# How 64-bit weights become 32-bit ones in the opening of a one-core light-convolution and maxout kernel: low bits on ScalarE or GpSimd

## The chip, the cores and the metric

One Trainium2 chip, one core, one program. The metric is device time in microseconds: before the change the median of 3 runs is 1399.69 us (1399.49 to 1399.96). PE is TensorE (PEld its weight loads), DVE is VectorE, ACT is ScalarE, POOL is GpSimd, SP is SyncE, which issues the DMAs.

## The reference

Two stages, one after the other. The first is a light convolution: for each of 8 x 4160 tokens and each of 8 heads, 7 weights go through a softmax and mix the token with the 6 before it (192 features, 24 per head). The second is a maxout layer: `h = max(x @ w1, x @ w2, x @ w3)` with 192 x 768 weights, then `out = h @ w_out` with 768 x 192. The four weight matrices come as 64-bit floats; tokens and convolution weights are 32-bit.

## The kernel before

**Tiling.** The 33,280 tokens are 65 chunks of 512, each 4 tiles of 128. 192 features are a first part of 128 rows (names with a) and a second part of 64 (names with b). 768 hidden features are 6 blocks `j`, taken as 3 pairs `jp`. Per chunk the kernel makes four tap products and their sums (`taps`: L522 on POOL or, for the tiles of TAPS_ON_VECTOR, on DVE; the sums L535 on DVE), turns the tokens so that features lie in the partitions, splits them into a high and a low part (`parts`), multiplies with the weights (`up`), takes the maximum (`evict`) and multiplies with w_out (`down`). So that the maximum needs only two products, x @ w1 is taken out of it and added at the end through a composed matrix `wc = w1 @ w_out` (`compose`); `up` uses the differences `w2 - w1` and `w3 - w1` (`differences_a`, `differences_b`), a relu (L1389) and a maximum (L1397, L1406).

**Two ways to multiply.** Chunk 0 uses full 32-bit matmuls (`up_whole`, L1349 and L1356; `down_whole`, L1436 to L1445), which need no split weights. From chunk 1 on, weights and tokens are high and low parts and the two halves of 64 rows of the array work side by side (`products`, L1287). The low parts of the weights are made by `rest` (L1004), of w_out at L1129; xb, a low part of the tokens, at L723.

**64-bit to 32-bit** (`single`, L814 on). Twelve pieces: for each pair ('a', jp, 0) with 256 columns (w1), ('a', jp, 1) with 512 (w2, w3), ('b', jp) with 384 (the last 64 rows of all three), and ('d', q) with 384 (w_out). ACT takes the high words' absolute value (L832) into a PSUM bank, or into a buffer `m` in SBUF if POOL clamps; a clamp follows, on DVE or POOL (L849) or as two scalings on ACT (L842); then three DVE passes: shift left by 3 (L856), join the sign from the high word (L865), join the low word shifted right by 29 (L874). In the last two, one input is the word in SBUF and the other the value in the bank:

```
nc.vector.scalar_tensor_tensor(
    target().bitcast(U32), low(), 29, ui(),
    op0=ALU.logical_shift_right, op1=ALU.bitwise_or,
)
```

**Last 64 rows.** `differences_b` writes the high part of a pair to `bhi` (L1089), in whose 128 partitions the even and the odd block lie in a half each, and four ACT copies (L1108) put each block into both halves of `wb_hi`, because both halves of the array need it.

**Composing.** `compose(0)` makes the first 128 rows of wc, `compose(1)` the last 64, each by six matmuls added up in one bank (L1181; each is recorded as two passes); copies on ACT (L1193, L1203, L1213, L1232) and a subtraction on DVE (L1220) make the parts.

**Order of the work.** The program is written by a planner in Python: each instruction is a task with an engine, a cost, predecessors, buffers it holds and a due time; per engine the ready task with the earliest time goes first. TensorE's tasks alone keep the order of the program. For chunks 0 and 1 that order is the list OPENING, written by hand: loads, softmax, conversions (`singles`), taps, 'warm' (matmuls of the identity, L898, each unit 128 columns, which fill the time until data is there), 'turn x' (tokens, L576, L613), 'turn' (weights, L1156, L1157), 'a' and 'b' (differences, L1017, L942), 'up', 'compose' and 'down'. LOAD_DUE sets when the loads are due, and a table of shifts in `Plan(...)` moves the times of single tasks. MODE, CLAMP_ON_POOL, CLAMP_ON_SCALAR and ON_POOL_FIRST say which engine makes a difference, a clamp or a low part.

## Time and profile before

| | |
|---|---|
| runs | 1399.69 us median of 3 (1399.49 to 1399.96) |
| profiled execution | 1399.97 us |
| its span, first to last instruction | 1398.1 us |
| granted clock of TensorE, mean | 0.999 |
| PE, PEld busy | 1391.6, 1327.1 us |
| DVE, ACT, POOL busy | 1009.5, 1128.3, 1094.8 us |

The page gives busy shares for the whole span; waits, timelines, windows and groups are asked of the trace for one engine or stretch. The end of a matmul is modelled, so of PE the starts are read, not the lengths. Times in a view count from the span's start.

### The profile page before, as it was taken

Reading aid. Unit: us, or ns where it says so; the run is one execution under the profiler, and the core shown is the slowest. Engines: PE = TensorE matmul, PEld = TensorE weight load, DVE = VectorE, ACT = ScalarE, POOL = GpSimd, SP = SyncE. Lnnn points to the kernel's source line nnn. Section 1 sums busy time; section 2 is a strip of 40 time slices with the busy share of each in tenths; the row PEclk is TensorE's granted clock in tenths of the full one; section 3 lists DMA queues with packets and bytes.
Section 4 is the critical chain, followed back from the end, with each engine's and each line's share of the span. In section 5 each row is a group of like instructions: output and inputs, shape, how many; then the busy total and the mean of one; then the engine's idle time right before and its main releaser. Section 6 shows DMA issues by size and latency. Waiting matters only on the chain.

```text
span 1398.1 us, 36944 instructions
## 1 busy us (share of the span) xinstructions
PE 1391.6 (100%) x14825; PEld 1327.1 (95%) x14825; DVE 1009.5 (72%) x1373; ACT 1128.3 (81%) x2870; POOL 1094.8 (78%) x606
## 2 busy tenths in 40 slices
PE   9999999999999999999999999999999999999998
PEld 4899999999999999999999999999999999999998
DVE  7988777677677678668668667668767768767533
ACT  6687888788888888888788888888888888789773
POOL 7999998788788788788788788788788788788321
PEclk9999999999999999999999999999999999999999
DMA  7202211011111011111011111011111111110000
GB/s 245 104 19 105 75 58 70 25 60 69 70 60 69 24 59 70 70 59 70 24 59 70 70 59 70 26 57 70 70 59 70 38 55 60 56 63 19 24 24 24
DMA packets 23532, 85.68 MB, mean 61 GB/s; under 512 B 2632, under 2 KB 9544, under 8 KB 19520
## 3 DMA queue, kind: packets, MB, share of 16 engines
q1 hardware_dynamic: 23360, 83.32, 16.2%
q8 instruction: 116, 1.90, 0.6%
q14 instruction: 56, 0.46, 0.1%
HBM read 57.75 MB, written 25.56 MB: 60 GB/s over the span
## 4 chain that ended last, share of the span: by engine, by line
PE 92%; DVE 2%; POOL 2%; ACT 1%; DMA 1%; issue 1%; SPq 0%; DVEq 0%; POOLq 0%; ACTq 0%
PE bank L1287 92%; POOL r L522 1%; DVE acc L535 1%; ACT room L688 1%; DMA h_lo<-in_moe_w_dram 0%; POOL h_lo L1417 0%; DMA h_hi<-in_moe_w_dram 0%; DVE h_hi L1397 0%; DVE bank L865 0%; DVE bank L856 0%; PE bank L1265 0%; ACT m L1389 0%; POOL xb L723 0%; POOL wt L485 0%; DVE r L522 0%
## 5 line engine op out<-in xcount | busy, mean ns | idle before, releaser
L522 POOL TENSOR_TENSOR r<-xt,wt 128x1344 f32<-128x1344 f32 x257 | 714.2, 2845 | 139.1 <-DVE acc L535 137.1
L1287 PE MATMUL bank<-wo,h_hi 64*128 64x384 f32 x3060 | 657.4, 356 | 0.0
L1287 PE MATMUL bank<-wo,h_lo 64*128 64x192 f32 x3060 | 584.5, 247 | 0.0
L688 ACT COPY room<-room 32x128 f32<-32x128 f32 x1512 | 448.6, 297 | 61.4 <-DVE room L677 38.3
L1287 PEld LDWEIGHTS bank<-wo,h_lo 64*128 64x128 f32 x3060 | 480.4, 187 | 0.0
L1287 PEld LDWEIGHTS bank<-wo,h_hi 64*128 64x128 f32 x3060 | 471.5, 185 | 0.0
L1287 PE MATMUL bank<-xa_hi,wa_hi 64*128 64x512 f32 x1536 | 459.0, 389 | 0.0
L1287 PE MATMUL bank<-xa_lo,wa_hi 64*128 64x512 f32 x1536 | 455.6, 387 | 0.0
L1287 PE MATMUL bank<-xa_hi,wa_lo 64*128 64x512 f32 x1536 | 455.1, 387 | 0.0
L535 DVE TENSOR_REDUCE acc<-r 128x192 f32<-128x1344 f32 x257 | 399.6, 1556 | 5.2 <-POOL r L522 4.3
L1287 PE MATMUL bank<-xc,wb_hi 64*128 64x512 f32 x768 | 276.8, 386 | 0.0
L1389 ACT ACTIVATE m<-bank 128x512 f32<-128x512 f32 x390 | 232.4, 597 | 54.3 <-PE bank L1287 48.5
L1287 PE MATMUL bank<-xb,wb_hi 64*128 64x512 f32 x768 | 271.6, 387 | 0.0
L1287 PE MATMUL bank<-xc,wb_lo 64*128 64x512 f32 x768 | 250.5, 386 | 0.0
L1287 PEld LDWEIGHTS bank<-xa_hi,wa_hi 64*128 64x128 f32 x1536 | 239.6, 184 | 9.1 <-issue 0.2
L1287 PEld LDWEIGHTS bank<-xa_lo,wa_hi 64*128 64x128 f32 x1536 | 239.5, 184 | 8.9
L1287 PEld LDWEIGHTS bank<-xa_hi,wa_lo 64*128 64x128 f32 x1536 | 238.9, 184 | 9.2
L1528 DVE TENSOR_TENSOR o<-bank,ob 128x192 f32<-128x192 f32 x255 | 89.0, 349 | 187.7 <-ACT ob L1521 187.5
L1417 DVE TENSOR_TENSOR h_lo<-bank,h_hi 128x512 fp32r<-128x512 f32 x254 | 174.1, 685 | 59.6 <-ACT h_hi L1410 59.1
L1417 POOL TENSOR_TENSOR h_lo<-m,h_hi 128x512 fp32r<-128x512 f32 x130 | 171.1, 1317 | 39.4 <-ACT h_hi L1410 39.2
L1406 DVE TENSOR_TENSOR bank<-bank,m 128x512 f32<-128x512 f32 x254 | 175.4, 691 | 16.2 <-ACT m L1389 10.3
L1287 PE MATMUL bank<-wca,xa_hi 64*128 64x384 f32 x510 | 179.4, 352 | 0.3 <-SPq L1293 0.3
(132 smaller groups left out, 2046.7 us busy)
## 6 DMA issues: line engine op xcount, KB each, us to landing
xt<-in_x_dram SPq DMA_DIRECT2D x30, 1344.0 KB, 5.8
out_dram<-o SPq DMA_DIRECT2D x64, 384.0 KB, 2.3
wt<-in_weight_gen_dram SPq DMA_DIRECT2D x31, 224.0 KB, 2.5
xt<-in_x_dram SPq DMA_DIRECT2D x2, 960.0 KB, 6.6
h_hi<-in_moe_w_dram SPq DMA_DIRECT2D x6, 256.0 KB, 4.6
xt<-in_x_dram SPq DMA_DIRECT2D x2, 768.0 KB, 5.0
room<-in_moe_w_out_dram SPq DMA_DIRECT2D x2, 384.0 KB, 6.9
h_lo<-in_moe_w_dram SPq DMA_DIRECT2D x6, 128.0 KB, 5.0
```

Source lines behind the costliest of these rows:

```text
L522: on.tensor_tensor(to, buf(hx)[:, la + t : la + t + K].rearrange("p k (h g) -> p k h g", g=G), wide() .rearrange("p (h k) -> p k h", k=K) ...
L535: pin(nc.vector.tensor_reduce(buf(ha)[:, t], of, axis=AX.X, op=ALU.add))
L688: pin(nc.scalar.copy(to[:, :, p : p + 32], b[p : p + 32, :, f : f + 32]))
L1287: ins = nc.tensor.matmul(buf(hb)[:, :n], w()[h], v()[h], start=half == 0 and first, stop=half == 1 and last,)
L1389: lambda: pin(nc.scalar.activation(buf(hm), buf(hb), AF.Relu)), [made], due,
L1406: lambda: pin(nc.vector.tensor_tensor(buf(keep), buf(hb), buf(hm), op=ALU.max)),
L1417: eng.tensor_tensor(buf(hl)[:, j], buf(keep), buf(hh)[:, j].bitcast(F32), op=ALU.subtract)
L1528: nc.vector.tensor_tensor(buf(ho)[:, t], buf(hb)[:, :D], buf(hq), op=ALU.add)
```

## The change

It touches the opening alone, but for one entry of TAPS_ON_VECTOR (chunk 3).

- Ten of twelve pieces are converted in a crossed form (ENDS). ACT's absolute value is scaled by 2^-112, one clamp from above is left (on POOL for ('a', 1, 0) and ('d', 1), else on DVE), and a pair like ('DVE', 'ACT') names who takes the sign and who the low word's upper bits. What ACT or POOL takes is read as one 16-bit part of the 64-bit word (by scale and bias or `tensor_scalar`) and written as an integer into `m` in SBUF; a sign on DVE is joined into it from the high word. One DVE pass shifts the clamped value and joins `m`. ('a', 2, 1) and ('b', 1) keep the old form, with the clamp on DVE.
- `wb_hi` is kept per pair, once as it comes and once with its halves exchanged; `bhi` goes, and two copies per pair are left of four.
- The second part of composing puts even j on the lower, odd j on the upper column half of the array; both sums are then added, with a copy of each on ACT in between.
- OPENING, LOAD_DUE, MODE, the clamp lists and the planner's shifts are new. The planner's limit of 8 loads in flight counts SP's loads alone; LOAD_ON_SCALAR is empty and TOGETHER is 0, so what they control does not run.

```diff
-    ON_POOL_FIRST = (0, 1, 2, 3)
-    TAPS_ON_VECTOR = ((0, 0), (2, 3), (3, 2))
+    ON_POOL_FIRST = (0, 5)
+    TAPS_ON_VECTOR = ((0, 0), (2, 3), (3, 1))
 
     MODE = {('a', 0): ('POOL', 'POOL'),
-         ('a', 1): ('POOL', 'DVE'),
-         ('a', 2): ('POOL', 'L'),
-         ('b', 0): ('POOL', 'POOL'),
+         ('a', 1): ('POOL', 'L'),
+         ('a', 2): ('POOL', 'POOL'),
+         ('b', 0): ('POOL', 'DVE'),
          ('b', 1): ('POOL', 'DVE'),
          ('b', 2): ('POOL', 'POOL')}
-    CLAMP_ON_POOL = (('a', 0, 0), ('a', 1, 0), ('a', 2, 0), ('b', 0))
-    CLAMP_ON_SCALAR = (('a', 0, 1), ('a', 1, 1), ('d', 0), ('d', 1), ('d', 2))
-    LOAD_DUE = {('a', 0): -99.9,
-         ('a', 1): -93.4,
-         ('a', 2): -90.9,
+    CLAMP_ON_POOL = (('a', 1, 0), ('d', 1))
+    CLAMP_ON_SCALAR = (('a', 0, 0), ('a', 0, 1), ('d', 2))
+    ENDS = {('a', 0, 0): ('DVE', 'ACT'),
+         ('a', 0, 1): ('DVE', 'ACT'),
+         ('a', 1, 0): ('DVE', 'ACT'),
+         ('a', 1, 1): ('POOL', 'ACT'),
+         ('a', 2, 0): ('DVE', 'ACT'),
+         ('b', 0): ('DVE', 'POOL'),
+         ('b', 2): ('POOL', 'POOL'),
+         ('d', 0): ('POOL', 'POOL'),
+         ('d', 1): ('POOL', 'ACT'),
+         ('d', 2): ('DVE', 'ACT')}
+    TOGETHER = 0
+    LOAD_DUE = {('a', 0): -97.4,
+         ('a', 1): -97.9,
+         ('a', 2): -95.9,
          ('b', 0): -97.4,
          ('b', 1): -96.4,
          ('d',): -86.4,
          ('s', 0): -96.4,
-         ('s', 1): -99.4}
+         ('s', 1): -96.9}
+    LOAD_ON_SCALAR = ()
...
+    MOST = float(np.array(0x0FEFFFFF, np.uint32).view(np.float32))
...
     OPENING = (('load b', 0, 1), ('load b', 1, 3), ('load a', 2), ('load', 0), ('load a', 0),
          ('load a', 1), ('load down',), ('load', 1), ('softmax', 0), ('softmax', 1), ('singles', 2),
-         ('singles', 0), ('singles', 1), ('singles down',), ('taps', 0), ('taps', 1), ('warm', 11),
-         ('warm', 1), ('warm', 1), ('warm', 1), ('warm', 2), ('warm', 18), ('turn x', 0, 3),
-         ('turn x', 0, 2), ('warm', 3), ('turn x', 0, 0), ('turn x', 0, 1), ('warm', 2),
-         ('warm', 1), ('warm', 4), ('warm', 1), ('turn', 0), ('warm', 4), ('parts', 0),
-         ('a', 0, 0, 1), ('a', 0, 1, 2), ('b', 0), ('up', 0, 0), ('a', 1, 0, 2), ('b', 1),
-         ('up', 0, 2), ('turn', 1), ('turn', 2), ('a', 2, 0, 2), ('b', 2), ('up', 0, 4),
-         ('compose', 1), ('compose', 0), ('turn x', 1, 2), ('turn x', 1, 0), ('turn x', 1, 1),
-         ('turn x', 1, 3), ('down', 0), ('parts', 1), ('up', 1, 2), ('up', 1, 1), ('up', 1, 0),
-         ('up', 1, 3), ('up', 1, 4), ('up', 1, 5))
+         ('singles', 0), ('singles', 1), ('singles down',), ('taps', 0), ('taps', 1), ('warm', 2),
+         ('warm', 8), ('warm', 18), ('warm', 4), ('warm', 4), ('warm', 3), ('warm', 4), ('warm', 2),
+         ('turn x', 0, 0), ('warm', 1), ('warm', 1), ('turn x', 0, 1), ('turn x', 0, 3),
+         ('turn x', 0, 2), ('warm', 1), ('turn', 0), ('warm', 4), ('turn', 2), ('parts', 0),
+         ('a', 0, 0, 1), ('a', 0, 1, 2), ('b', 0), ('up', 0, 0), ('warm', 1), ('turn', 1),
+         ('a', 1, 0, 2), ('b', 1), ('up', 0, 2), ('compose', 1), ('a', 2, 0, 2), ('b', 2),
+         ('up', 0, 4), ('turn x', 1, 0), ('compose', 0), ('turn x', 1, 1), ('turn x', 1, 3),
+         ('warm', 1), ('turn x', 1, 2), ('down', 0), ('parts', 1), ('up', 1, 2), ('up', 1, 3),
+         ('up', 1, 0), ('up', 1, 4), ('up', 1, 1), ('up', 1, 5))
...
-    wb_hi = const.tile([P, NJ, NI, P], F32R, name="wb_hi")
+    wb_hi = const.tile([P, NP, 2, NI, P], F32R, name="wb_hi")
...
+        crossed = key in ENDS
+        if crossed:
+            by_scalar, (sign_on, low_on) = False, ENDS[key]
+        hm = hold("m")
+        of_x = lambda: like(buf(hm)[:, :n])
+
+        def half(at):
+            v = buf(hm)[:, :n].bitcast(U16)
+            if len(source().shape) == 3:
+                return v.rearrange("p (n w) -> p n w", w=2)[..., at]
+            return v.rearrange("p (i n w) -> p i n w", n=source().shape[2], w=2)[..., at]
+
+        def of_words(on, of, to, a, b, one, two, deps):
+            scaled = lambda: to(), lambda: source().bitcast(U16)[..., of]
+            if on == "ACT":
+                return plan.add(
+                    "ACT", act_near(n),
+                    lambda: pin(nc.scalar.activation(to(), scaled[1](), AF.Copy, scale=a, bias=b)),
+                    deps, None, [hm, hc, *holds],
+                )
+            return plan.add(
+                "POOL", 0.16 + 0.00093 * n,
+                lambda: pin(
+                    nc.gpsimd.tensor_scalar(to(), scaled[1](), a, b, op0=one, op1=two)
+                ),
+                deps, None, [hm, hc, *holds],
+            )
+
+        def ends_of():
+            got = []
+            whole_word = sign_on == "DVE"
+            if sign_on == "ACT":
+                got.append(
+                    plan.add(
+                        "ACT", act_near(n),
+                        lambda: pin(
+                            nc.scalar.activation(
+                                of_x(), high().bitcast(F32), AF.Copy, scale=0.0, bias=-0.0
+                            )
+                        ),
+                        deps, None, [hm, hc, *holds],
+                    )
+                )
+            elif sign_on == "POOL":
+                got.append(
+                    of_words(
+                        "POOL", 3, lambda: half(1), 2.0**15, 2.0**15, ALU.is_ge, ALU.mult, deps
+                    )
+                )
+            if low_on != "DVE":
+                to = (lambda: of_x().bitcast(U32)) if whole_word else (lambda: half(0))
+                got.append(
+                    of_words(
+                        low_on, 1, to, 2.0**-13, 2.0**-14 - 0.5, ALU.mult, ALU.add,
+                        [*deps, *(got if sign_on == "ACT" else [])],
+                    )
+                )
+            if "DVE" in (sign_on, low_on):
+                of, a, op = (low, 29, ALU.logical_shift_right) if low_on == "DVE" else (
+                    high, 0x80000000, ALU.bitwise_and
+                )
+                got = [
+                    plan.add(
+                        "DVE", vec(n),
+                        lambda: pin(
+                            nc.vector.scalar_tensor_tensor(
+                                of_x().bitcast(U32), of(), a, of_x().bitcast(U32),
+                                op0=op, op1=ALU.bitwise_or,
+                            )
+                        ),
+                        [*deps, *got], None, [hm, hc, *holds],
+                    )
+                ]
+            return got
...
-                    u(), high().bitcast(F32), AF.Abs, scale=2.0**111 if by_scalar else 1.0
+                    u(), high().bitcast(F32), AF.Abs, 
+                    scale=2.0**-112 if crossed else 2.0**111 if by_scalar else 1.0,
...
+        elif crossed:
+            b = plan.add(
+                "POOL" if by_pool else "DVE", (0.16 + 0.00093 * n) if by_pool else vec(n),
+                lambda: pin(eng.tensor_scalar(u(), u(), MOST, None, op0=ALU.min)),
+                [a], None, [hu],
+            )
...
+        if crossed:
+            x = ends_of()
+            return plan.add(
+                "DVE", vec(n),
+                lambda: pin(
+                    nc.vector.scalar_tensor_tensor(
+                        target().bitcast(U32), u().bitcast(U32), 3, of_x().bitcast(U32),
+                        op0=ALU.logical_shift_left, op1=ALU.bitwise_or,
+                    )
+                ),
+                [b, *x], None, [hb, hu, hc, hm],
+            )
...
-        hq = hold("bhi")
+        own = lambda: wb_hi[:, jp, 0]
...
-            b_hi[2 * jp + odd] = [
-                plan.add(
-                    "ACT", 0.42,
-                    lambda to=to, h=h, odd=odd: pin(
-                        nc.scalar.copy(wb_hi[to, 2 * jp + odd], buf(hq)[h].bitcast(F32))
-                    ),
-                    [e], None, [hq],
-                )
-                for to in halves
-            ]
+            copied = plan.add(
+                "ACT", 0.42,
+                lambda to=halves[1 - odd], h=h: pin(
+                    nc.scalar.copy(wb_hi[to, jp, 1], own()[h].bitcast(F32))
+                ),
+                [e], None, [],
+            )
+            b_hi[2 * jp + odd] = [(e, copied)[other] for other in ((0, 1) if odd == 0 else (1, 0))]
...
+    def compose_low():
+        hb, ht = hold("bank"), hold("m")
+        deps = [turned_w[j] for j in range(NJ)] + [o_32[j] for j in range(NJ)]
+        below, above = halves
+
+        def mult():
+            for j in range(NJ):
+                pin(
+                    nc.tensor.matmul(
+                        buf(hb)[halves[j % 2], :D], w1t()[:, j, P:], wo32[:, j],
+                        start=j < 2, stop=j >= NJ - 2,
+                    )
+                )
+
+        got = whole(1.15, mult, deps, [hb, hw1t])
+        crossed = [
+            plan.add(
+                "ACT", act(D),
+                lambda to=to, of=of: pin(nc.scalar.copy(buf(ht)[to, :D], buf(hb)[of, :D])), [got],
+                clock[0] + 0.5, [hb, ht],
+            )
+            for to, of in ((above, below), (below, above))
+        ]
+        both = plan.add(
+            "DVE", vec(D),
+            lambda: pin(
+                nc.vector.tensor_tensor(buf(hwc)[:, 1, :D], buf(hb)[:, :D], buf(ht)[:, :D], op=ALU.add)
+            ),
+            crossed, clock[0] + 0.7, [hb, ht, hwc],
+        )
+        of_c32.append(both)
...
+        if n == 1 and WHOLE_DOWN:
+            return compose_low()
...
+            w_b = lambda: wb_hi[:, jp, int(half != odd), i]
```

## Rows read from the trace of the kernel before

**Rows 1.** The page: busy time of each engine.
```profile
PE 1391.6 (100%) x14825; PEld 1327.1 (95%) x14825; DVE 1009.5 (72%) x1373; ACT 1128.3 (81%) x2870; POOL 1094.8 (78%) x606
```

**Rows 2.** Waits of TensorE in the whole run: us in total, times, longest.
```profile
PE bank L1349 <- POOL h_lo L1017: 0.8, 1, 0.8
PE bank L898 <- ACT xa_hi L637: 0.5, 1, 0.5
```

**Rows 3.** Timeline of TensorE, the opening: start us, us, instructions.
```profile
19.97 1.02 PE L898 MATMUL bank<-ident 128*128 128x512 f32 x2
20.83 1.88 PE L1349 MATMUL bank<-xa_hi,h_lo 128*128 128x512 f32 x4
...
27.77 1.98 PE L1349 MATMUL bank<-xa_hi,h_lo 128*128 128x512 f32 x4 [0.82 <-POOL h_lo L1017]
...
33.72 0.44 PE L1156 MATMUL bank<-ident,w1a 128*128 128x128 f32 x2
...
34.42 1.88 PE L1349 MATMUL bank<-xa_hi,h_lo 128*128 128x512 f32 x4
...
40.27 4.31 PE L1181 MATMUL bank<-wo,raw 128*64 128x192 f32 x24
44.42 0.27 PE L613 MATMUL bank<-ident,acc 128*128 128x128 f32 x1
...
45.07 0.27 PE L613 MATMUL bank<-ident,acc 128*128 128x128 f32 x1
...
45.29 0.49 PE L1436 MATMUL bank<-wx,xa_hi 128*128 128x192 f32 x2
...
55.78 0.47 PE L1287 MATMUL bank<-xb,wb_hi 64*128 64x512 f32 x1
```

**Rows 4.** Stretches of the opening: us, each engine's busy us, PEclk, DMA share, GB/s.
```profile
16.00:24.00 8.00, 7.50 (x34) 4.14 (x33) 6.59 (x16) 6.20 (x15) 4.95 (x8) 1.00 1.05 305
24.00:40.00 16.00, 15.18 (x46) 5.12 (x44) 16.00 (x28) 15.22 (x38) 15.92 (x13) 1.00 0.32 127
40.00:55.00 15.00, 15.00 (x94) 13.71 (x92) 15.00 (x15) 4.93 (x14) 14.79 (x9) 1.00 0.29 108
```

**Rows 5.** DVE groups by shape, 0 to 56 us: busy us, mean ns, idle before.
```profile
L865 DVE SCALAR_TENSOR_TENSOR bank<-h_lo,bank 128x384 uint32<-128x384 uint32 x4 | 2.2, 554 | 0.0
...
L865 DVE SCALAR_TENSOR_TENSOR bank<-h_hi,bank 128x512 uint32<-128x512 uint32 x2 | 1.4, 688 | 0.0
...
L865 DVE SCALAR_TENSOR_TENSOR bank<-h_hi,bank 128x256 uint32<-128x256 uint32 x2 | 0.8, 425 | 0.0
...
L1004 DVE TENSOR_TENSOR wa_lo<-h_lo,wa_hi 128x512 fp32r<-128x512 f32 x1 | 0.8, 818 | 0.0
L1004 DVE TENSOR_TENSOR wb_lo<-b,bhi 128x256 fp32r<-128x256 f32 x1 | 0.8, 818 | 0.0
```

**Rows 6.** Timeline of DVE, 40 to 56 us.
```profile
41.99 1.28 DVE L1397 TENSOR_TENSOR h_hi<-bank,m 128x512 f32<-128x512 f32 x2
43.19 3.01 DVE L535 TENSOR_REDUCE acc<-r 128x192 f32<-128x1344 f32 x2
...
55.03 0.67 DVE L723 TENSOR_TENSOR xb<-bank,xc 64x512 fp32r<-64x512 f32 x1
```

**Rows 7.** POOL groups by shape, 0 to 56 us.
```profile
L522 POOL TENSOR_TENSOR r<-xt,wt 128x1344 f32<-128x1344 f32 x12 | 31.3, 2653 | 2.1 <-DMA xt<-in_x_dram 1.8 <-DVE acc L535 0.2
...
L1129 POOL TENSOR_TENSOR wo<-wo,wo 128x384 fp32r<-128x384 f32 x2 | 2.2, 1084 | 0.0
L1004 POOL TENSOR_TENSOR wa_lo<-h_lo,wa_hi 128x512 fp32r<-128x512 f32 x1 | 1.7, 1724 | 0.0
...
L849 POOL TENSOR_SCALAR m<-m 128x384 f32<-128x384 f32 x1 | 0.5, 506 | 0.0
```

**Rows 8.** ACT groups by shape, 0 to 56 us.
```profile
L1108 ACT CAST wb_hi<-bhi 64x256 fp32r<-64x256 f32 x12 | 4.8, 402 | 0.2
...
L842 ACT ACTIVATE bank<-bank 128x384 f32<-128x384 f32 x6 | 2.8, 474 | 0.0
```

More of the change, by code (lines that the diff above doesn't have):

```diff
@@ L13 @@
 U32 = mybir.dt.uint32
+U16 = mybir.dt.uint16
 AF = mybir.ActivationFunctionType
@@ L781, in load_b @@
         got = []
+        by, on = queue_of(("b", first))
         for i, w in enumerate(words[:3]):
@@ L794, in load_b @@
                         ),
-                        (), LOAD_DUE["b", first], [hraw[2]], issue=0.62,
+                        (), LOAD_DUE["b", first], [hraw[2]], on=on, issue=0.65,
                     )
@@ L1088, in differences_b @@
         e = plan.add(
-            "ACT", act(2 * P), lambda: pin(nc.scalar.copy(buf(hq), v())), [d], None, [*holds, hq]
+            "ACT", act(2 * P), lambda: pin(nc.scalar.copy(own(), v())), [d], None, holds
         )
@@ L1170, in turn_weights @@
             turned_w[j] = out
+    def compose_low():
[27 more added lines that the diff above has]
+        of_c32.append(both)
+        hi = plan.add(
+            "ACT", act(D), lambda: pin(nc.scalar.copy(wcb[:, :D], buf(hwc)[:, 1, :D])), [both],
+            clock[0] + 1.5, [hwc],
+        )
+        lo = plan.add(
+            "DVE", vec(D),
+            lambda: pin(
+                nc.vector.tensor_tensor(
+                    wcb[:, D:], buf(hwc)[:, 1, :D], wcb[:, :D].bitcast(F32), op=ALU.subtract
+                )
+            ),
+            [hi], clock[0] + 2, [hwc],
+        )
+        of_c.extend((hi, lo))
     def compose(n):
+        if n == 1 and WHOLE_DOWN:
+            return compose_low()
         for to, f in (((wca, slice(0, P)), (wcb, slice(P, D)))[n],):
@@ L1321, in terms @@
                 (
-                    (CH, lambda: wb_hi[:, j, i], lambda: buf(b), [*b_hi[j], bl], [b])
+                    (CH, w_b, lambda: buf(b), [b_hi[j][half], bl], [b])
                     if half == low
-                    else (CH, lambda: wb_hi[:, j, i], lambda: buf(k), [*b_hi[j], *cs], [k])
+                    else (CH, w_b, lambda: buf(k), [b_hi[j][half], *cs], [k])
                 ),
@@ L1385, in evict @@
         hh, hl, his, los = hs[c]
+        if whole_h and TOGETHER:
+            hs[c, j, i] = hb, made
+            if i == 1:
+                h0, made0 = hs[c, j, 0]
+                his[j] = plan.add(
+                    "DVE", vec(CH) + TOGETHER,
+                    lambda: pin(
+                        nc.vector.scalar_tensor_tensor(
+                            buf(hh, None, F32)[:, j], buf(hb), 0.0, buf(h0), op0=ALU.max,
+                            op1=ALU.max,
+                        )
+                    ),
+                    [made, made0], due, [hb, h0, hh],
+                )
+            return
         if i == 0:
```

28 lines of the change are left out of this document (15 added, 13 removed), and 26 rows, old and new, of the table plan.

## The prediction

> **What bounds the kernel now.** I read the page first: TensorE is busy for 1391.6 of 1398.1 us, the three others between 72% and 81% [rows 1]. A busy TensorE may hide slow matmuls, so the waits of TensorE come next: in the whole run it waits twice for data that this change can reach, 0.8 us for a difference of the second weight pair and 0.5 us for ACT's copy of the first tokens [rows 2]. From the first L1287 product at 55 us on, its work is the same before and after. So the change can only pay in the opening, and the timeline of TensorE says what that consists of: 'up' of chunk 0 from 20.83, composing from 40.27, 'down' of chunk 0 from 45.29, the ordinary products from just before 55.78 [rows 3]. Last the windows: DVE has no free time at all from 24 to 55 us and POOL next to none, while ACT is idle for ten of the fifteen us from 40 to 55 [rows 4]. Two lists, TensorE's and DVE's, run beside each other without slack and meet twice: DVE starts the sums of chunk 1's last tokens at 43.19 and TensorE turns the last of them at 45.07; DVE makes xb from 55.03 and TensorE takes it at 55.78 [rows 3, 6]. An edit shortens the run only as far as it shortens both.
>
> **TensorE's list.** One unit of warm-up costs (20.83 - 19.97) / 4 = 0.215 us [rows 3]. The new list has 52 units ahead of the first 'up' where the old one has 49: +0.65. One pair of turned weights comes ahead of it as well; two pairs took 34.42 - 33.72 = 0.70, so +0.35. The 0.5 us wait for ACT goes, if the longer list covers the copies: -0.5. The first 'up' starts at 20.83 + 0.65 + 0.35 - 0.5 = 21.33. From there to 'down' it took 45.29 - 20.83 = 24.46 us. Out of this go the 0.8 us wait (the second pair's turned weights and a warm unit now stand in front of that 'up', but the list arrives there about 27.4 to 28, and the difference was ready at 27.77, so I count it gone), the pair of turned weights that was moved ahead (0.35), and half of one composing; in come two warm units (0.43).
>
> Composing takes 44.42 - 40.27 = 4.15 us for both parts, 2.07 each [rows 3]. The new second part has the same products, but even and odd j go to different column halves of the array. No row of before shows two column halves at work together, so its price lies between 2.07 (they take turns) and 1.04 (side by side), or a little above 2.07 if going from half to half costs something, of which there is no row either. The nearest rows are L1287's products on two row halves, which the timeline shows running side by side; I take 1.04. TensorE's list then changes by +0.5 at the front and -0.8 - 0.35 - 1.03 + 0.43 = -1.75 behind it: **-1.3 us** at the start of 'down'.
>
> **DVE's list.** A 64-bit word becomes 32 bits by clamping, shifting, taking the sign and taking the low bits. DVE did three or four passes per piece; the crossed form needs one to three. Counted over MODE, ENDS and the clamp lists: for 256 columns 9 passes become 8, for 512 columns 10 become 9, for 384 columns 20 become 15. At 0.425, 0.688 and 0.554 us [rows 5] that is 0.43 + 0.69 + 2.77 = 3.9. Back to back a pass costs 0.09 less than its length (two of 0.685 in 1.28 us [rows 6]), which makes 3.3. Composing adds one sum of 192 columns, under the 0.425 of 256: +0.35. The low part of w_a pair 1 goes from DVE to POOL, that of w_b pair 0 comes the other way; both were 0.818 [rows 5]: nothing. That is -2.9.
>
> Against it stands how the new passes read. The old ones joined a word in SBUF with a bank in PSUM. Eight of the new ones have both inputs in SBUF: the sign passes of a00, a01, a10, a20, b0 and d2, and the last passes of a10 and d1, whose clamped value lies in SBUF. The only such passes of before are the two of L1004: 0.818 for 512 columns against 0.688 for a pass with one input in a bank, and 0.818 for 256 against 0.425 [rows 5]. So a pass pays between 0.13 and 0.39 more in these rows; I take the middle, 0.26, since the new ones lie between and at both sizes: +2.1. DVE's list changes by **-0.8 us**. It could be none (-2.9) if POOL stands still at those moments, or several us, which is the third rival.
>
> **ACT and POOL.** ACT loses ten scalings (0.474 us for 384 columns) and gains seven passes over low halves of about that size, which start from SBUF like its first pass; it loses six of twelve copies of 0.402 [rows 8]. That is some 4 us less, and it costs or gives nothing at once, since DVE is behind it. POOL gets seven passes over 16-bit halves: between 0.506 (its clamp of 384 columns) and 1.084 (a two-input pass of 384) each [rows 7]; they have one input, so I take 0.506, one of them 512 wide: 3.7. It also gets the low part of w_a pair 1, up to 1.72, and gives up the clamps of two 256 pieces and w_b's low part, some 1.5. Sum +3.9. Of this 3.05 us are free between 16 and 24 us [rows 4], and the low parts can follow later. At 1.084 each the sum would be +8, of which four or five us would push chunk 1's products back.
>
> The loads issue no more DMAs than before, in another order on the same SP queue: pair 0's first, pair 1's and the tokens of chunk 1 around them. TensorE's list starts the first token's turn later than before, so I count nothing for it. The order ('up', 1, ...) and ON_POOL_FIRST act beside a TensorE that is busy anyway: two low parts of chunk 1 move from POOL to DVE, behind the meeting points. The last rows' copies and the new layout of wb_hi change neither a matmul's shape nor its count.
>
> **The sum.** The smaller of -1.3 and -0.8 is what both lists allow: -0.8 us. The profiled execution took 1399.97 us, 1.9 more than its span, and stands 0.28 above the median of 1399.69; the terms carry over to the median: 1398.9.
>
> **Rivals.**
> The first: TensorE's list decides alone, because the eight passes fall where POOL is waiting. Then DVE gains up to 2.9 and the run -1.3, with the few tenths by which the first pair's groups were slower than the second's -1.5: 1398.2 to 1398.4. For it: POOL has 3 us free from 16 to 24 us [rows 4]. Against it: none after 24.
>
> The second: the change does not do what it says in composing, and the column halves take turns. TensorE's list then changes by -0.3, and the run with it: 1399.4. The page TensorEngine Tiling (Array Packing) of the Trainium skill (Key Properties) says that a change of the tiling mode drains the engine and that column tiles run independently of each other; no run here shows either for columns. The row halves of L1287 speak for running side by side.
>
> The third ends slower: DVE and POOL lock each other out. Place: the eight passes with two SBUF inputs. The two such passes of before lasted 0.818 each though one is twice as wide [rows 5], so it was not their width that set it. If such a pass has to wait for the whole POOL instruction that is under way, it waits half of a tap product on average, 2.65 / 2 = 1.3 us [rows 7]. If four of eight meet one and four meet a shorter pass (half of some 0.8), that is 4 x 1.3 + 4 x 0.4 = 6.8 in place of 2.1; DVE's list changes by 6.8 - 2.9 = +3.9, of which a us may fall into its gaps before 22 us. The run takes 1402.6. From 2.9 / 8 = 0.36 us per pass on there is no gain, and from 0.71 on it is slower by over 0.2%. The page SBUF — State Buffer of the Trainium skill (SBUF: two separate sides) states this rule: a DVE instruction with two SBUF inputs and a GpSimd instruction that reads SBUF hold the shared port one at a time, each for the whole instruction. That the two passes of before are stretched to one length agrees with it, and by it alone the third rival would be the forecast; what speaks against its full price is that half of the passes stand early, where DVE still has gaps.
>
> **Chances.** The forecast, gain of 0.4 to 1.2: 0.45. First rival: 0.22. Second: 0.13. Third: 0.20, of which half is under 0.2% slower. A measurement of this kernel can tell about 0.2% (2.8 us) from no change. Faster than that would need more than TensorE's list has to give: 0.03. Slower than that: 0.10. Within: 0.87. The range reaches down to the first rival with the spread of the runs shown, 1397.5, and up to the milder half of the third, 1401.6.
>
> **What the profile would show.** Right: the first L1349 at about 21.3, no wait for L1017's difference, L1181's products in about 3.1 us in place of 4.15, 'down' at 44 to 44.5, ten L842 gone, and new DVE passes of 0.5 to 0.8 us. Wrong: new waits of TensorE for DVE's sums or POOL's products between 27 and 70 us; sign passes of over a us on DVE; 16-bit passes of a us on POOL; L1181 still over 4 us.

## The result and the profile after

The changed kernel took **1407.95 us** (median of 6 runs, 1407.6 to 1408.64) beside 1399.97 us for the kernel before in the same measurement: a ratio of 1.0057, 95% interval 1.0044 to 1.007. It is 8.0 us slower; I had predicted 0.8 us faster, with a range that ended at 1401.6. The profiled execution has a span of 1405.8 us against 1398.1. All ratios here leave out two executions in the chip's slower state, 1775.32 us of the kernel before and 1915.62 us of the last experiment's kernel.

The waits of TensorE from 15 to 75 us in the changed kernel (us in total, times, longest):

```profile
PE bank L1510 <- POOL h_lo L1131: 3.3, 2, 2.8
PE bank L1012 <- DVE wo L960: 1.7, 1, 1.7
PE bank L1269 <- DVE b L960: 0.7, 1, 0.7
PE bank L1447 <- DVE xb L738: 0.4, 1, 0.4
```

The one wait that I had counted gone [rows 2] has become the largest. Line 1510 is the 'up' of chunk 0 (L1349 before), 1131 the difference of w_a on GpSimd (L1017 before). The timeline of TensorE shows where the time goes:

```profile
21.42 1.98 PE L1510 MATMUL bank<-xa_hi,h_lo 128*128 128x512 f32 x4 [0.46 <-POOL h_lo L1131]
...
32.76 3.78 PE L1510 MATMUL bank<-xa_hi,h_lo 128*128 128x512 f32 x4 [2.79 <-POOL h_lo L1131]
...
38.48 2.02 PE L1510 MATMUL bank<-xa_hi,h_lo 128*128 128x512 f32 x4
...
41.49 1.20 PE L1293 MATMUL bank<-wo,raw 128*64 128x192 f32 x12
42.62 1.99 PE L1510 MATMUL bank<-xa_hi,h_lo 128*128 128x512 f32 x4
...
51.95 0.54 PE L1612 MATMUL bank<-wx,xa_hi 128*128 128x192 f32 x2
...
63.05 0.50 PE L1447 MATMUL bank<-xb,wb_hi 64*128 64x512 f32 x1 [0.36 <-DVE xb L738]
```

The first 'up' starts at 21.42 (predicted: 21.33). The second pair's 'up' starts at 32.76 where it stood at 27.77 before [rows 3]: 5.0 us late. 'down' starts 6.7 us late (51.95 against 45.29), the product with xb 7.3 us late (63.05 against 55.78), and the span is 7.7 us longer. Nearly all of it is lost in the opening. The windows show one thing more (us, busy us of PE, PEld, DVE, ACT, POOL, then PEclk):

```profile
24.00:40.00 16.00, 11.49 (x29) 3.95 (x25) 10.74 (x15) 8.38 (x19) 13.61 (x11) 0.79 0.27 106
...
32.00:38.00 6.00, 5.24 (x8) 1.68 (x8) 5.96 (x7) 2.85 (x7) 4.29 (x3) 0.50 0.01 1
```

Between 24 and 40 us DVE, which had no free time before [rows 4], is idle for 5.3 us. TensorE, which had been busy for 1.25 of the 5 us from 27 to 32, shows a granted clock of 0.50 (1.2 of 2.4 GHz) from 32 to 38 us, so that its first 'up' group there takes 5.7 us (32.76 to 38.48) instead of 3.0. The groups of GpSimd from 10 to 56 us, its timeline, and the timeline of DVE:

```profile
L867 POOL TENSOR_SCALAR m<-room 128x384 uint16<-128x384 uint16 x3 | 3.9, 1300 | 0.2
...
L867 POOL TENSOR_SCALAR m<-h_hi 128x512 uint16<-128x512 uint16 x1 | 2.4, 2364 | 0.1
L867 POOL TENSOR_SCALAR m<-h_lo 128x384 uint16<-128x384 uint16 x2 | 2.3, 1168 | 0.1
...
L945 POOL TENSOR_SCALAR m<-m 128x384 f32<-128x384 f32 x1 | 1.2, 1172 | 0.1
...
L867 POOL TENSOR_SCALAR m<-h_lo 128x384 uint32<-128x384 uint16 x1 | 0.9, 871 | 0.1
L945 POOL TENSOR_SCALAR m<-m 128x256 f32<-128x256 f32 x1 | 0.9, 856 | 0.1
```

```profile
22.14 1.64 POOL L867 TENSOR_SCALAR m<-room 128x384 uint16<-128x384 uint16 x1
...
31.44 1.26 POOL L1131 TENSOR_TENSOR h_lo<-wx,w1a 128x512 f32<-128x512 f32 x1
```

```profile
13.16 2.48 DVE L909 SCALAR_TENSOR_TENSOR m<-h_hi,m 128x512 uint32<-128x512 uint32 x2
...
27.19 0.69 DVE L960 SCALAR_TENSOR_TENSOR wx<-bank,m 128x512 uint32<-128x512 uint32 x1 [1.41 <-POOL m L867]
...
31.51 1.61 DVE L960 SCALAR_TENSOR_TENSOR wo<-m 128x384 uint32<-128x384 uint32 x1 [2.41 <-POOL m L945]
...
34.37 2.13 DVE L1118 TENSOR_TENSOR wb_lo<-b,wb_hi 128x256 fp32r<-128x256 f32 x1
```

The seven passes of L867 take 3.9 + 2.4 + 2.3 + 0.9 = 9.5 us; I had put them at 3.7. The groups with means of 1300 and 1168 ns mix two kinds: one by one, a sign of 384 columns took 1.64 to 1.71 us and low bits 0.62. The two clamps, which have lost one of their two operations, take 1.17 and 0.86; with both, 384 columns took 0.506 [rows 7]. DVE waits for both kinds, and the second pair's difference stands behind them in GpSimd's list: it starts at 31.44, and in the kernel before it started at 26.44.

```profile
26.44 1.27 POOL L1017 TENSOR_TENSOR h_lo<-wx,w1a 128x512 f32<-128x512 f32 x1
```

Two suspects were left: GpSimd's own passes, and passes on DVE with both inputs in SBUF, of which some last several times what their width asks for (2.13 us for 256 columns).

### The profile page after: what moved, and what is told of

Read it like the earlier page. It is cut to its first block, busy times and chain, and to the rows that moved or that the text cites. A ratio compares the mean times of both kernels' runs of the same rounds, so it can differ in the third digit from the quotient of the medians.

```text
span 1405.8 us, 36942 instructions
## 1 busy us (share of the span) xinstructions
PE 1394.4 (99%) x14827; PEld 1333.5 (95%) x14827; DVE 1011.3 (72%) x1369; ACT 1124.8 (80%) x2860; POOL 1103.7 (79%) x609
## 4 chain that ended last, share of the span: by engine, by line
PE 94%; DVE 2%; ACT 1%; POOL 1%; SPq 1%; DMA 1%; issue 0%; DVEq 0%; ACTq 0%
PE bank L1447 94%; DVE acc L550 1%; POOL m L867 0%; DMA xt<-in_x_dram 0%; ACT room L703 0%; SPq L808 0%; DMA room<-in_moe_w_out_dram 0%; PE bank L1425 0%; SPq L454 0%; DVE wb_lo L1118 0%; POOL b L1056 0%; POOL m L945 0%; DVE h_hi L1573 0%; DVE wo L960 0%; DVE r L537 0%
## 5 line engine op out<-in xcount | busy, mean ns | idle before, releaser
L1447 PE MATMUL bank<-wo,h_hi 64*128 64x384 f32 x3060 | 648.5, 355 | 0.0
L1447 PE MATMUL bank<-xa_hi,wa_hi 64*128 64x512 f32 x1536 | 497.0, 389 | 0.2 <-DVE h_lo L1593 0.2
L1447 PE MATMUL bank<-xa_lo,wa_hi 64*128 64x512 f32 x1536 | 493.3, 387 | 0.0
L1447 PE MATMUL bank<-xa_hi,wa_lo 64*128 64x512 f32 x1536 | 492.5, 386 | 0.0
L1447 PEld LDWEIGHTS bank<-wo,h_lo 64*128 64x128 f32 x3060 | 473.7, 187 | 0.0
L1447 PE MATMUL bank<-xc,wb_hi 64*128 64x512 f32 x768 | 288.7, 386 | 0.0
L1447 PE MATMUL bank<-xc,wb_lo 64*128 64x512 f32 x768 | 272.4, 386 | 0.0
L1447 PEld LDWEIGHTS bank<-xa_lo,wa_hi 64*128 64x128 f32 x1536 | 263.6, 184 | 7.8
L1447 PEld LDWEIGHTS bank<-xa_hi,wa_lo 64*128 64x128 f32 x1536 | 263.0, 184 | 7.6
L1447 PEld LDWEIGHTS bank<-xa_hi,wa_hi 64*128 64x128 f32 x1536 | 260.1, 184 | 8.9 <-DVE h_lo L1593 0.6
```

The lines of the kernel that those rows point to most:

```text
L1447: ins = nc.tensor.matmul(buf(hb)[:, :n], w()[h], v()[h], start=half == 0 and first, stop=half == 1 and last,)
```

## The experiments

The first three give the sign and the low bits to other engines. They change engines and costs, so the planner, whose shifts are kept by task number, wrote a new order for the opening.

**No 16-bit pass on GpSimd.** The four pieces with a sign on POOL, and b0, get ('DVE', 'ACT'). (b0 is the piece ('b', 0), a11 the piece ('a', 1, 1), and so on.)

```diff
-         ('a', 1, 1): ('POOL', 'ACT'),
-         ('b', 0): ('DVE', 'POOL'),
-         ('b', 2): ('POOL', 'POOL'),
-         ('d', 0): ('POOL', 'POOL'),
-         ('d', 1): ('POOL', 'ACT'),
+         ('a', 1, 1): ('DVE', 'ACT'),
+         ('b', 0): ('DVE', 'ACT'),
+         ('b', 2): ('DVE', 'ACT'),
+         ('d', 0): ('DVE', 'ACT'),
+         ('d', 1): ('DVE', 'ACT'),
```

> The changed kernel with ENDS ('DVE', 'ACT') for all ten pieces: POOL has none of its seven 16-bit passes (L867, 8.6 us in the changed kernel up to 56 us), DVE gets five more sign passes with both inputs in SBUF. Theory 1 (POOL's 16-bit passes are late and everything behind them on POOL and DVE waits): the second pair's difference is ready by 28, TensorE waits under 1 us for it, its clock stays at 2.4 GHz, and the run takes 1399 to 1401. Theory 2 (the DVE passes with two SBUF inputs and POOL lock each other out): there are more of them, so 1407 to 1411. Theory 3 (the new list and order of loads are what is late): no change, 1407 to 1409.

Measured: 1404.48 us, ratio 1.0033 (1.002 to 1.0046), between the ranges of the first two theories. (The seven passes of the changed kernel take 9.5 us, not 8.6, and DVE gets four more sign passes, not five, since b0's sign was there already.) No wait for GpSimd is left; DVE is busy for all 16.00 us from 24 to 40, and TensorE waits for it:

```profile
PE bank L1293 <- DVE wo L960: 2.1, 1, 2.1
PE bank L1269 <- DVE b L960: 1.7, 1, 1.7
```

So without these passes on GpSimd, and with four of them on DVE, the run is 3.5 us faster than the changed kernel, and TensorE now waits for DVE. How much of this is the passes and how much the new order, this run doesn't separate.

**Sign and low bits on ScalarE.** All ten pieces get ('ACT', 'ACT').

```diff
-    ENDS = {('a', 0, 0): ('DVE', 'ACT'),
...
+    ENDS = {('a', 0, 0): ('ACT', 'ACT'),
...
```

> The changed kernel with ENDS ('ACT', 'ACT') for all ten pieces: ACT takes sign and low bits, POOL has no 16-bit pass and DVE no sign pass; of passes with two SBUF inputs only the last ones of ('a', 1, 0) and ('d', 1) are left. ACT has ten passes more than with ('DVE', 'ACT'), some 5 us, where it was idle for 7 of 16 us (24 to 40 us of the changed kernel). Theories 1 and 2 alike: 1398.5 to 1400.5; if theory 2 counts beside theory 1, it is over 0.5 us faster than all ten on ('DVE', 'ACT'). Theory 3: 1407 to 1409.

Measured: 1418.83 us, ratio 1.0134 (1.0119 to 1.015), outside every range. (The weights made this way are not the reference's, so that only the time is read.) The new order lets DVE begin the next chunk's sums ahead of the last sum of chunk 1, and TensorE stands for it:

```profile
PE bank L628 <- DVE acc L550: 8.8, 1, 8.8
```

This says nothing about the passes; it says how little an order tuned for other engines is worth.

**The old conversion, the rest of the change kept.**

```diff
-    CLAMP_ON_SCALAR = (('a', 0, 0), ('a', 0, 1), ('d', 2))
-    ENDS = {('a', 0, 0): ('DVE', 'ACT'),
...
+    CLAMP_ON_SCALAR = ()
+    ENDS = {}
```

> The changed kernel with the old way of converting all twelve pieces (three joining passes on DVE, clamps on DVE but for ('a', 1, 0) and ('d', 1) on POOL); wb_hi by half, the composing on two column halves, list and loads stay as changed. DVE has 10 passes more than in the changed kernel, some 5 us, none of them with two SBUF inputs. Theories 1 and 2: the 8 us come back for the most part, less what DVE's passes cost, 1400 to 1403. Theory 3: 1407 to 1412.

Measured: 1418.64 us, ratio 1.0133 (1.0118 to 1.0148), outside every range too, and again by the order: GpSimd takes tap products at 26.89 and 30.65 us (5.16 us for two) ahead of a difference at 35.68, and TensorE waits 7.6 us.

```profile
PE bank L1501 <- POOL h_lo L1122: 7.6, 1, 7.6
```

From here on the kernel's own order is kept (that of the changed kernel, or in one run of the kernel before), but for what a diff says.

**32-bit words on GpSimd.** The seven passes read and write whole words, with the same operations; they no longer make the right bits.

```diff
-                    nc.gpsimd.tensor_scalar(to(), scaled[1](), a, b, op0=one, op1=two)
+                    nc.gpsimd.tensor_scalar(of_x(), high().bitcast(F32), a, b, op0=one, op1=two)
```

> The changed kernel, POOL's seven passes with the same two operations, but from the 32-bit high word to a 32-bit word (the converted weights of b0, b2, a11, d0, d1 are not the reference's). It separates the 16-bit access from the operation: if 16-bit access made the sign passes 1.64 us for 384 columns and 2.36 for 512, they fall to 0.5 to 0.7 and the run to 1400 to 1402; if the comparison does, they stay above 1.5 and the run stays at 1406 to 1409. The passes for low bits, 0.62 in the changed kernel where nothing held them up, stay at 0.5 to 0.65 either way.

Measured: 1408.2 us, ratio 1.0058 (1.0043 to 1.0073). The operations of L867 on GpSimd (times, then shortest, median and longest ns):

```profile
L867 POOL TENSOR_SCALAR m<-room x3: 529/1527/1528, 22.3 to 28.9; 128x384 f32<-128x384 f32 x3
L867 POOL TENSOR_SCALAR m<-h_hi x1: 2200/2200/2200, 24.9 to 24.9; 128x512 f32<-128x512 f32 x1
```

The passes of a sign still take 1.53 us for 384 columns in this group, the one of low bits 0.53. It is not the 16-bit access.

**Other operations, same place.** Sign passes take a product and a sum in place of a comparison and a product (the signs of a11, b2, d0 and d1 are lost); clamps take a minimum and a maximum in place of a minimum alone.

```diff
-                        "POOL", 3, lambda: half(1), 2.0**15, 2.0**15, ALU.is_ge, ALU.mult, deps
+                        "POOL", 3, lambda: half(1), 1.0, 0.0, ALU.mult, ALU.add, deps
...
-                lambda: pin(eng.tensor_scalar(u(), u(), MOST, None, op0=ALU.min)),
+                    eng.tensor_scalar(u(), u(), MOST, 0.0, op0=ALU.min, op1=ALU.max)
```

> The changed kernel in its own order; only two operations on POOL are others: its four sign passes multiply and add in place of comparing and multiplying (the signs of b2, a11, d0, d1 are lost), its two clamps get a second operation, a maximum with 0, which changes no value. If the operations are what is slow on POOL, the sign passes fall from 1.64 (384 columns) and 2.36 (512) to 0.62 and 0.8, the clamps from 0.86 and 1.17 to 0.40 and 0.51, some 5.3 us in all. Theory 1 (POOL's slow passes make the second pair's difference late): TensorE's wait for it falls from 2.8 to under 0.5, its clock stays up, and the run takes 1400 to 1402. Theory 2 (DVE's passes with two SBUF inputs): 1406 to 1408. Theory 3 (list and loads): 1407 to 1409.

Measured: **1402.82 us**, ratio 1.0024 (1.0015 to 1.0034). Two of the groups of GpSimd, and two lines of TensorE's timeline:

```profile
L867 POOL TENSOR_SCALAR m<-room 128x384 uint16<-128x384 uint16 x3 | 1.9, 629 | 0.2
...
L867 POOL TENSOR_SCALAR m<-h_hi 128x512 uint16<-128x512 uint16 x1 | 0.8, 767 | 0.1
```

```profile
28.04 1.98 PE L1512 MATMUL bank<-xa_hi,h_lo 128*128 128x512 f32 x4 [0.26 <-POOL h_lo L1133]
...
33.63 3.68 PE L1512 MATMUL bank<-xa_hi,h_lo 128*128 128x512 f32 x4 [2.56 <-DVE wx L990]
```

The seven passes fall to 5.1 us (9.5 in the changed kernel), the clamps to 1.1 (2.0), and the second pair's 'up' starts at 28.04. Of 8.0 us of loss 5.2 are GpSimd's choice of operations (8.0 less the 2.8 that are left here). The sign passes are now near the price that I had assumed, and the run is still 2.8 us above the kernel before. What is left shows as a new wait, for a bank that the last pass of the piece in the old form (a, 2, 1) frees on DVE.

**DVE's sign passes with one input from SBUF.** They no longer join the low bits that lie in `m`.

```diff
-                            nc.vector.scalar_tensor_tensor(
-                                of_x().bitcast(U32), of(), a, of_x().bitcast(U32),
-                                op0=op, op1=ALU.bitwise_or,
+                            nc.vector.tensor_scalar(
+                                of_x().bitcast(U32), of(), 0, a,
+                                op0=ALU.logical_shift_left, op1=ALU.bitwise_and,
```

> The changed kernel in its own order; only DVE's six sign passes read one input from SBUF, not two (the low bits that ACT or POOL wrote are lost there). They fall from 5.3 us in all to 3.1. Theory 1: 1407 to 1408, at most 1 us less than the changed kernel. Theory 2: 1401 to 1404. Theory 3: no change.

Measured: 1408.15 us, ratio 1.0059 (1.0044 to 1.0074). The passes did get shorter (two in 1.29 us, in place of 2.48 above), and the time did not:

```profile
14.06 1.29 DVE L909 TENSOR_SCALAR m<-h_hi 128x512 uint32<-128x512 uint32 x2
```

**Both of the last two edits at once.**

> The two edits together (signs and low bits as there). If the two slow kinds of passes are the whole of it, the run takes what the lists gave without them, 1398.4 to 1400, and TensorE has no wait over 0.5 us after the identity. If it stays over 1402, something else of the change is late, and the waits left show what.

Measured: 1402.79 us, ratio 1.002 (1.001 to 1.0029), as with GpSimd's edit alone, and over 1402: something else is late. The sign passes on DVE cost this kernel nothing.

**TensorE kept busy ahead of the second pair.** Fourteen products of the identity fill its wait.

```diff
+            for _ in range(14 if jp == 1 else 0):
+                pin(nc.tensor.matmul(buf(hb)[:, 2 * D :], ident, ident, start=True, stop=True))
```

> The changed kernel in its own order; TensorE gets 14 more matmuls of the identity (128 columns each, 3.0 us at 2.4 GHz) ahead of the second pair's turned weights, where it waits for the difference anyway. If its clock fell because it stood idle, the first 'up' of that pair takes 3.0 us in place of 5.7 and the run 1405 to 1405.7; if the fall has another cause, 1407.5 to 1408.5.

Measured: 1408.09 us, ratio 1.006 (1.0043 to 1.0077). TensorE's timeline here, and a line of DVE's in the changed kernel:

```profile
30.09 4.92 PE L1268 MATMUL bank<-ident 128*128 128x128 f32 x28
...
35.17 1.88 PE L1512 MATMUL bank<-xa_hi,h_lo 128*128 128x512 f32 x4
...
38.97 2.01 PE L1512 MATMUL bank<-xa_hi,h_lo 128*128 128x512 f32 x4 [0.86 <-DVE wx L988]
```

```profile
37.63 0.67 DVE L988 SCALAR_TENSOR_TENSOR wx<-raw,bank 128x512 uint32<-128x512 uint32 x1
```

'Up' now runs at full speed (granted clock 1.00 from 35 to 38 us), as it would if the fall came from standing idle, but the time that this was to save is not saved: 'up' starts 2.4 us later behind the fourteen, and its second group waits for DVE at 38.97 where it had started at 38.48. In the changed kernel that same pass of DVE ended at 38.30, and the second group started at 38.48: the slow clock lay beside this wait and cost 0.2 us of its own at most.

**One low part on DVE issued later.** On top of the edited GpSimd passes (signs lost), the subtraction of 2.13 us goes behind the last pass of (a, 2, 1). 183 and 83 are their task numbers.

```diff
+    listed = plan.order()
+    late = next(t for t in listed if t.n == 183)
+    listed.remove(late)
+    listed.insert(next(k for k, t in enumerate(listed) if t.n == 83) + 1, late)
...
```

> The kernel with the fast GpSimd passes (signs of four pieces lost, clamps with two operations), whose time was 1402.8, with one more edit: on VectorE the subtraction that makes a low part of the last rows' weights (2.14 us beside GpSimd's tap product, where the same subtraction took 0.50 later) is issued behind the last pass of the one piece in the old form for which TensorE waited 2.6 us. Nothing else in any engine's order is moved. Theory 1, the rest of the loss lies in VectorE's list, where passes with two inputs in SBUF stand beside GpSimd's: the piece's last pass starts by about 31.8 instead of 32.91, TensorE's wait falls from 2.6 us to 1.4 or less, and the time to 1400.0 to 1401.7. Theory 2, what comes behind (third pair's difference on GpSimd, composing, 'down') is late by itself: the wait falls but the first products start within 0.5 us of 58.4 and the time stays at 1402.3 to 1403.0.

Measured: 1404.14 us, ratio 1.0028 (1.0018 to 1.0039): 1.3 us slower than without the move, and outside the times of both theories. The wait of 2.6 us fell to 0.6, as the first theory said, but the first products started at 59.07 us, later than 58.40. TensorE's new wait, two lines of DVE and one of GpSimd:

```profile
PE bank L628 <- DVE acc L550: 2.7, 1, 2.7
```

```profile
31.36 0.42 DVE L1120 TENSOR_TENSOR wb_lo<-b,wb_hi 128x256 fp32r<-128x256 f32 x1
...
36.76 2.73 DVE L1120 TENSOR_TENSOR wb_lo<-b,wb_hi 128x256 fp32r<-128x256 f32 x1
```

```profile
36.64 5.38 POOL L537 TENSOR_TENSOR r<-xt,wt 128x1344 f32<-128x1344 f32 x2
```

The moved subtraction takes 0.42 us in its new place. But the other low part on DVE, 0.50 us before this move, now begins just after a tap product on GpSimd and ends at 39.49, when the first of the two (half of 5.38 us) is over. So in this trace the loss has moved to another pass of the same kind; the last experiment takes both away.

**Column halves alone, on the kernel before.** Every engine's order is that of before; `over` is a buffer of its own.

```diff
+                    for j in range(NJ):
+                        pin(
+                            nc.tensor.matmul(
+                                buf(hb)[halves[j % 2], :D], w1t()[:, j, f], wo32[:, j],
+                                start=j < 2, stop=j >= NJ - 2,
+                            )
+                        )
...
```

> The kernel before, with every engine's order kept, and of the change only the second part of composing on two column halves (two copies on ScalarE and an addition on VectorE put both sums together). Theory 1, the change's gain on TensorE's list: the twelve passes take 1.13 us instead of 2.07, 'down' starts 0.9 us earlier, and the time is 1398.9 to 1399.3 beside 1400.0 for the kernel before. Rival: what 'down' and the second chunk's tokens wait for is set by other engines, so that the time stays within 0.3 us of the kernel before; or the longer chain of copies and addition ends behind the first chunk's 'down' and the time rises by up to 0.6 us.

Measured: 1401.21 us (11 runs) beside 1400.15, ratio 1.0007 (0.9998 to 1.0016). A gain of 0.9 us would be 0.9994, outside the interval; the rival's times are inside it. TensorE's timeline, DVE's and GpSimd's:

```profile
40.67 1.20 PE L1195 MATMUL bank<-wo,raw 128*64 128x192 f32 x12
...
57.21 0.49 PE L1316 MATMUL bank<-xb,wb_hi 64*128 64x512 f32 x1 [1.10 <-DVE xb L724]
```

```profile
45.06 0.34 DVE L1256 TENSOR_TENSOR wx<-bank,over 128x192 f32<-128x192 f32 x1
...
49.28 1.24 DVE L1260 TENSOR_TENSOR wcb<-wx,wcb 128x192 fp32r<-128x192 f32 x1
```

```profile
45.21 5.20 POOL L523 TENSOR_TENSOR r<-xt,wt 128x1344 f32<-128x1344 f32 x2 [0.20 <-DVE acc L536]
```

The twelve passes end at 41.79 where composing goes on: 1.12 us instead of 2.07. But DVE's list grows by the addition (0.34) and by a subtraction that now has both inputs in SBUF, lies beside tap products and takes 1.24 us (L1220 of the kernel before, with one input in a bank, 0.34). Those 1.24 us stand ahead of xb, and TensorE waits 1.10 for it. A shorter list of TensorE had next to nothing to gain there to begin with: in the kernel before DVE's xb ended at 55.70 and TensorE took it at 55.78 [rows 3, 6].

**A sign without a comparison.** As the kernel with the subtraction moved, with the signs made again.

```diff
-                        "POOL", 3, lambda: half(1), 1.0, 0.0, ALU.mult, ALU.add, deps
+                        "POOL", 3, lambda: half(1).bitcast(I16), 0.0, 2.0**15, ALU.min, ALU.mult, deps
```

> As the kernel with the subtraction behind the last pass, but GpSimd's sign passes do their work again, without a comparison: the high part is read as a signed 16-bit number, the smaller of it and 0 is taken and multiplied by 2^15. Theory 1, the comparison alone was dear: these passes take 0.5 to 0.9 us for 384 columns instead of 1.64 to 1.71, and the time is within 1 us of the kernel with the signs lost. Rival: any pass that makes a sign on GpSimd costs as much (1.5 us or more for 384 columns), and the time goes back to 1405 or more.

Measured: 1408.05 us, ratio 1.0056 (1.0043 to 1.0069).

```profile
L868 POOL TENSOR_SCALAR m<-room 128x384 int16<-128x384 int16 x2 | 3.5, 1774 | 0.2
L868 POOL TENSOR_SCALAR m<-h_hi 128x512 int16<-128x512 int16 x1 | 2.3, 2347 | 0.1
```

The first theory falls: it is not the comparison alone. A minimum with a product is as dear (one by one 1.63, 1.71 and 1.91 us for 384 columns); a product with a sum and a minimum with a maximum are the cheap pairs seen here.

**A sign from a product and a sum, and both low parts on GpSimd.** x times 0.0 plus -0.0 is a zero with the sign of x; as bfloat16 its bits are the sign alone. The two subtractions go to GpSimd, behind the last tap product of chunk 1 (task 152).

```diff
+                        "POOL", 3, lambda: half(1).bitcast(BF16), 0.0, -0.0, ALU.mult, ALU.add, deps
...
+    low_engine = {183: nc.gpsimd, 201: nc.gpsimd}
...
+    at = listed.index(taken[152]) + 1
+    listed[at:at] = [taken[183], taken[201]]
...
```

> The changed kernel's order with three edits. GpSimd's sign passes take a product with 0.0 and the addition of -0.0 instead of a comparison and a product: the high part read as a signed 16-bit number gives a zero with its sign, written as bfloat16, whose one set bit is the sign. GpSimd's clamps have a minimum and a maximum. The two subtractions on VectorE that make low parts of the last rows' weights are done by GpSimd instead, behind the last tap product of the second chunk, where GpSimd stood idle for 1.47 us. Theory 1, GpSimd has a fast way for a product with an addition whatever the numbers: the sign passes take 0.55 to 0.75 us for 384 columns; rival: they take 1.5 us or more as every pass that made a sign so far, and the time is 1405 or more. Theory 2, what is left of the loss is VectorE's list in the opening, beside GpSimd's tap products above all (the two subtractions took 0.42 and 2.73 us in the kernel with one of them moved, whose time was 1404.1): TensorE's wait of 2.7 us for the fourth tile's sum falls under 0.5, the first products start by 56.5 us instead of 59.07, and the time is 1400 to 1401.7. Rival: something else ends last there, the first products start after 58 us, and the time stays above 1402.5.

Measured: **1400.61 us** (11 runs) beside 1399.76, ratio 1.001 (1.0001 to 1.0019). This is the whole change with all of its computation, called the mended kernel below: by the medians 0.85 us above the kernel before in place of 8.0. GpSimd's sign passes, TensorE's 'down' and its product with xb, and DVE's xb:

```profile
L869 POOL TENSOR_SCALAR m<-room 128x384 bf16<-128x384 int16 x2 | 1.3, 632 | 0.1
L869 POOL TENSOR_SCALAR m<-h_hi 128x512 bf16<-128x512 int16 x1 | 0.9, 943 | 0.0
```

```profile
44.41 0.55 PE L1620 MATMUL bank<-wx,xa_hi 128*128 128x192 f32 x2
...
55.76 0.49 PE L1455 MATMUL bank<-xb,wb_hi 64*128 64x512 f32 x1 [0.61 <-DVE xb L740]
```

```profile
55.06 0.65 DVE L740 TENSOR_TENSOR xb<-bank,xc 64x512 fp32r<-64x512 f32 x1
```

Both theories hold. The wait of 2.7 us is gone, 'down' starts at 44.41, and the clock of 24 to 40 us is 1.00. TensorE's product with xb starts at 55.76, before it was 55.78; DVE's xb at 55.06, before 55.03 [rows 3, 6].

## Why the prediction was wrong

**The step that failed** is the term of POOL: seven passes at "0.506 ... they have one input, so I take 0.506", bounded above by 1.084, summed with a low part and the clamps to 3.9 us and counted at nothing. Both halves of it were wrong. The price does not go by the number of inputs but by the pair of operations. The row that I took, a clamp with a minimum and a maximum, is one of the cheap pairs; a comparison with a product took 1.64 to 1.71 us for 384 columns and 2.36 for 512, outside my bounds. The same holds for the two clamps that lost an operation, a cost that I did not look at: 2.0 us in place of 1.1 with both operations. And the cover was no cover: I set free time of 16 to 24 us against the sum of the passes, but asked what is queued behind them only in the one sentence on 1.084 each. It was the second pair's difference, which started on GpSimd at 31.44 instead of 26.44, and TensorE's 'up' moved by the same 5.0 us. With cheap operations in the same places the loss fell by 5.2 us. My own sign for this, "16-bit passes of a us on POOL", came true; the chance that I gave it was too small, because no rival had that mechanism.

A second term failed beside it: the low parts on DVE, set off against each other as "nothing". Against the forecast the changed kernel lost 8.8 us (8.0 slower in place of 0.8 faster). GpSimd's operations are 5.2 of them, the two low parts with their places 1.9 (2.8 down to 0.85), and 1.7 are left in the mended kernel.

**The third rival** had the right mechanism at the wrong place. DVE passes with two SBUF inputs are held up beside GpSimd's instructions: 0.42 and 2.73 us for one shape in one kernel. That agrees with the rule of the Trainium skill that I had cited (SBUF — State Buffer, SBUF: two separate sides): such a pass and a GpSimd instruction that reads SBUF take the shared port in turn, each for its whole length. But the eight passes that I priced cost the run nothing as far as they were tried (the six sign passes read one input from SBUF, and the time stayed at 1408.15, and at 1402.79 with GpSimd's edit); the low parts did. Taking both off DVE is the step from 1402.8 to 1400.6. That run changed the places on both engines together; how the 2 us divide between shorter passes and a shorter list was not tried.

**TensorE's list** came out near its sum, in part by luck. Ahead of the first 'up' at 21.42 (21.33 predicted) stand two waits that I had not counted, 0.75 us for DVE's b and 0.46 for the first difference, and the rest of the list up to there was 1.1 us shorter than my sum. The other signs came true: composing in 1.13 + 1.95 = 3.08 us (3.1), 'down' at 44.41 in the mended kernel (44 to 44.5). The second rival falls: column halves ran side by side, and the Trainium skill's statement that column tiles run independently of each other (TensorEngine Tiling (Array Packing), Key Properties) agrees with 1.13 us in place of 2.07. But the shorter list bought nothing, on the kernel before as little as in the mended one: both times TensorE waited for DVE's xb (1.10 and 0.61 us). There I had expected 0.8 us of gain; the mended kernel shows none (55.06 against 55.03). So the rule "an edit shortens the run only as far as it shortens both" was right, and DVE's list was the one that I had too short. With GpSimd's passes and clamps near the price that I assumed and nothing else changed, the forecast would have been 3.6 us too low (2.8 slower in place of 0.8 faster), and it is 1.7 too low for the mended kernel. The subtraction in composing's second part, which now has both inputs in SBUF (1.17 us in the changed kernel, 0.34 before), was missing from my count of such passes.

**ACT** was counted at nothing, and no wait of TensorE names it. **The clock** fell to half, which I had not considered; here it lay beside another wait, as the run with fourteen more products shows.

What stays open is the last 0.85 us between the mended kernel and the one before (by the ratio 1.4, interval 0.1 to 2.7). Up to xb the two traces are level; behind it, where I had counted nothing, TensorE's weight loads wait twice in the mended kernel and not at all in the kernel before (56 to 76 us):

```profile
PEld bank L1455 <- DVE h_lo L1601: 0.5, 1, 0.5
PEld bank L1455 <- SPq L1461: 0.5, 1, 0.5
```

The 'down' of chunk 1 then starts at 74.99 against 74.02. The first wait is for a low part of chunk 1 on DVE, where the new ON_POOL_FIRST makes four of the six in place of two. No run took that entry back, so that the cause is not shown.

## What to carry to other kernels

Take the price of a GpSimd pass from a row with the same pair of operations, and if there is none, leave the upper end open: even the dearest row per column shown of the kernel before (1.72 us for 512 [rows 7]) would have given 1.3 us for 384 columns, where 1.64 to 1.71 were measured. Dropping an operation can make a pass dearer. For every pass that is added to an engine with free time, name the next instruction in its list that TensorE waits for, and work out its start again with the new passes in front. Where two engines' lists meet without slack, as here, an edit on one of them was worth nothing until the other was shorter, and the DVE subtractions with two SBUF inputs were short only where GpSimd had no long instruction under way.

## What the runs showed of the hardware

- GpSimd, one input, 384 columns: product and sum mostly 0.62 to 0.64 us (single passes up to 0.87), minimum and maximum 0.51, minimum alone 1.17, comparison and product 1.64 to 1.71, minimum and product 1.63 to 1.91. 32-bit words in place of 16-bit ones made little difference (1.53 to 1.60 for comparison and product, mostly 0.53 for a product and a sum).
- A product with 0.0 and the sum with -0.0 keeps the sign on GpSimd, so that a sign bit costs 0.63 us for 384 columns.
- A DVE subtraction of 256 columns with two SBUF inputs took 0.42 us by itself and 2.13 to 2.73 when it began during a tap product on GpSimd, ending about 0.2 us behind it.
- Twelve 32-bit passes of TensorE onto two column halves took 1.13 us, on one half 2.07.
